# Joining the even and odd key offsets of an attention feature tile in one group of column-tiled matmuls

## The chip, the cores and the metric

The kernel runs on one NeuronCore of a Trainium2 chip. The metric is the device time of one execution in microseconds, as a median over runs. The engines are named as in the profile: PE (TensorE, the matmuls), PEld (its weight loads), DVE (VectorE), ACT (ScalarE), POOL (GpSimd) and SP (SyncE, which issues most DMAs).

## What is computed

Two blocks alternate twice, on x of 2048 positions by 1024 features, each with a residual and a layer norm in front:

```python
x = x + A(layernorm(x))        # attention
x = x + B(layernorm(x))        # MLP over positions
x = x + A(layernorm(x))
x = x + B(layernorm(x))
```

A is attention over a dilated sliding window. It has 32 heads of 32 features, and position s looks at s, s-2, ..., s-14 alone:

```python
qkv = x @ wqkv                                      # [2048, 3*1024]
idx = pos[:, None] - 2 * arange(8)[None, :]         # negative: masked
logits = einsum("bhsd,bhswd->bhsw", q, k[idx]) * 32 ** -0.5
o = einsum("bhsw,bhswd->bhsd", softmax(logits), v[idx])
return o @ wo
```

B mixes positions: u = gelu(h^T w1 + b1) with 3584 hidden units, then y = u w2 + b2, transposed back.

## The kernel before, in words

**Staging.** The window steps by two, so even and odd positions never meet. The kernel splits the positions in two *classes* c of SC = 1024. Each pair of A and B is a *layer* here (li = 0, 1). q, k and v are held transposed, 128 features by 1024 positions: a *feature tile* dt, of which a class has 8. Four feature tiles make a *score group* n, so that a layer has groups 0 to 3 (class 0: 0 and 1; class 1: 2 and 3), and a group is worked on in two halves of two feature tiles.

**Scores, qk() (L434).** There is no matmul of q with k, since every position has its own 8 keys. For a feature tile, DVE multiplies q by four shifted windows of k at once (L444), giving T of 128 x 4096. The 8 offsets need two such products, called *parities* par: one for the even, one for the odd offsets of the window. TensorE then sums the 32 features of each head with a 0/1 matrix sel (L449): 8 matmuls that use 128 rows and 32 columns of the array, four of them side by side (*column-tiled*), for each product. They add into sc, two PSUM banks, one a parity. A *run* in this document is an unbroken sequence of them on PE, with ordinary 128x128 matmuls on either side.

```python
T = tpl.tile([P, 4, SC], BF16, name="T", tag="T")
nc.vector.tensor_tensor(out=T[:], in0=q..., in1=window(k, par, 2, ...), op=ALU.mult)
for sb in range(SB):
    for gr in range(4):
        nc.tensor.matmul(self.sc[32 * gr:32 * gr + 32, par], lhsT=sel[...], rhs=T[...], ...)
```

T shares the two buffers of pool tpl with pr, the intermediate of the value product.

**Softmax and values.** softmax_front() (L453) copies sc to L, adds the mask, takes the maximum and the exponential; softmax_back() (L463) sums, divides (Pb, L470) and writes Pb to DRAM. spread() (L479) reads it back, replicated over the 32 features of a head, as pb, by DMAs on POOL's queue. pv() (L489) multiplies pb by windows of v (L505), adds the 8 offsets (L509, L511), and leaves oT.

**Projections.** proj() (L395) makes a half of q, k or v of a feature tile with 8 matmuls of 128 x 512 (L412); ACT moves the result out of PSUM (L416, L419), k and v into a buffer with a shifted second copy. Weights come through SP's queue: wq tiles with three buffers (pool wqp), and wv, wo, w1 and w2 tiles with five (pool wbp). PSUM has six banks for ordinary products and the two of sc.

**Output projection and MLP.** out_proj() (L611) multiplies oT by wo in 128 x 512 blocks (i: row block, 0 to 7; n: column half), inside multiply() (L631); DVE adds the residual (L652, L655), and ACT or DVE norms the row block into h. Class 0 runs with early = 0, each block finished before the next; class 1 with early = 3: three row blocks are begun with the first six feature tiles and wait in their banks. gemm1() (L672) contracts over positions (L682), for class 0 first as *partials* (kept in the g buffers, L688), later with class 1's half added (L693). gemm2_tile() (L697) makes the output rows (L706), and in between layers also the next layer's normalised hb and its transposed hT.

**Buffers g.** The 14 buffers g0 to g13 hold gemm1's result, 28 hidden tiles, two in a buffer. The last eight, g6 to g13, hold v of class 1 until attention is done. g0 to g5 are 128 x 2048 and idle during the score work of layer 0's groups 1 and 2; g0 to g3 take x rows at the start.

**What sets the order.** Every engine works through a fixed list. The list follows the order in which weave() (L755) asks for units of work. A *lead* stream (stream(), L514) goes through the groups: products and runs, softmax, the next projections, the value products of the group before. *Fills* (second: the class-1 input rows; v_ahead: class 1's v; out0: class 0's output projection; partials, late: gemm1 of class 0) are put in wherever the planner thinks that PE would otherwise wait. The planner keeps two clocks, pe and dve. A unit of kind "dve" adds its cost to dve; if it has a following PE cost, fills are pulled until pe has reached dve. SLACK is 0.5 us; while class 0's output projection is open, a fill is also pulled for every OUT0_GAP = 7 us of DVE work as long as pe < dve + AHEAD. In qk(), a unit is one parity: 2.2 us of DVE, then 0.6 of PE. Instructions of one engine that are given different priorities are ordered by them, so the final list is not exactly the planner's; a wait on PE holds all that is behind it.

Of the kernel before, what the change touches and what calls it, by code (L numbers as in the profile page):

```python
# [11 lines left out]
ALU = mybir.AluOpType  # L12
FP32 = mybir.dt.float32
BF16 = mybir.dt.bfloat16

P = 128
H = 32
DH = 32
W = 8
# [7 lines left out]
def kernel(  # L27
# [13 lines left out]
    nc = tc.nc  # L41
    x_in = A_x[0]
    out2d = out[0]
    S, D = x_in.shape
    F = B_w1.shape[1]
    KD = D // P
# [20 lines left out]
    PB_LAG = 12.0  # L67
    PDW = 4 * SB * W * TB + 512
    OUT0_GAP = 7.0
    AHEAD = 10.0  # L70
    assert D == H * DH and W == 8 and SC == 1024 and HD * KD == H and SB * CH == 32
    scale = float(DH) ** -0.5

# [17 lines left out]
    class at:  # L91
# [8 lines left out]
        def __exit__(self, *a):  # L100
            self.c[0] = tc.cur_priority
            tc.cur_priority = self.old

    tc.cur_priority = 10_000_000
    top = [1_000_000]
# [59 lines left out]
    L = pers.tile([P, W, TB], FP32, name="L")  # L165
    m4 = pers.tile([P, 4, TB], FP32, name="m4")
    Pb = pers.tile([P, W, TB], BF16, name="Pb")
    g_raw = [pers.tile([P, 2 * KW if n >= NFB - KD else GF * D], BF16, name=f"g{n}") for n in range(NFB)]
    g = [t[:, 0:GF * D].rearrange("p (f d) -> p f d", d=D) for t in g_raw]
    v_g = [t[:].rearrange("p (r k) -> p r k", k=KW) for t in g_raw[NFB - KD:]]  # L170

    xa = [[dram.tile([SC, D], BF16, name=f"xa{li}{c}") for c in range(DIL)] for li in range(2)]
    xb = [dram.tile([SC, D], BF16, name=f"xb{c}") for c in range(DIL)]
# [13 lines left out]
    def window(t, par, off, shape):  # L187

        base = t[:, par, off]
        return bass.AP(base.tensor, base.offset, [base.ap[0]] + shape)  # L190
# [161 lines left out]
    class Attn:  # L352

        def __init__(self, li, hT, early):
            self.li, self.hT, self.early = li, hT, early
            self.oT = [[None] * KD for _ in range(DIL)]
            self.wts = {}
            self.pbs = {}

        def v_of(self, c, dt):  # L360
            return v_g[dt] if c else v_t[dt % 2]
# [72 lines left out]
        def qk(self, n, dq):  # L434
            c, dt = n // NCQ, (n % NCQ) * DQ + dq
            if dq == 0:
                self.sc = pssp.tile([P, 2, 4, TB], FP32, name="sc", tag="sc")
            q, k = self.q_of(c, dt), self.k_of(c, dt)
            for par in range(2):
                yield "dve", 2.2, [("ready", 0, dt), ("ready", 1, dt)], [("free", x, dt % 2) for x in range(2)] if par and not self.apart(c, dt) else [], 0.0, 0.6 * bool(n)  # L440
                if n == 0:
                    yield "pe", 0.6, [], [], 0.0
                T = tpl.tile([P, 4, SC], BF16, name="T", tag="T")
                nc.vector.tensor_tensor(out=T[:], in0=q.unsqueeze(1).to_broadcast([P, 4, SC]),  # L444
                                        in1=window(k, par, 2, [(2, 4), (1, SC)]), op=ALU.mult)
                for sb in range(SB):
                    for gr in range(4):
                        b = SB * gr + sb
                        nc.tensor.matmul(self.sc[32 * gr:32 * gr + 32, par], lhsT=sel[:, sb * DQ + dq, :],  # L449
                                         rhs=T[:, :, b * TB:(b + 1) * TB],  # L450
                                         start=(dq == 0 and sb == 0), stop=(dq == DQ - 1 and sb == SB - 1))

        def softmax_front(self):  # L453
            yield "dve", 4.5, [], ["exp"], 1.2, 0.0
# [8 lines left out]
        def softmax_back(self, n):  # L463
            yield "dve", 3.0, ["exp"], [("pb", n, 0)], PB_LAG, 0.0
            yield "dve", 0.0, [], [("pb", n, 1)], PB_LAG + 6.0, 0.0
            nc.vector.tensor_tensor(out=m4[:], in0=L[:, 0:4, :], in1=L[:, 4:8, :], op=ALU.add)
            nc.vector.tensor_tensor(out=m4[:, 0:2, :], in0=m4[:, 0:2, :], in1=m4[:, 2:4, :], op=ALU.add)
            nc.vector.tensor_tensor(out=m4[:, 0, :], in0=m4[:, 0, :], in1=m4[:, 1, :], op=ALU.add)
            nc.vector.reciprocal(out=m4[:, 1, :], in_=m4[:, 0, :])
            nc.vector.tensor_tensor(out=Pb[:], in0=L[:], in1=m4[:, 1:2, :].to_broadcast([P, W, TB]), op=ALU.mult)  # L470
            base = self.pd(n)[0, 0]
            dst = bass.AP(base.tensor, base.offset, [(W * TB, 4 * SB), (PDW, CH), (1, W * TB)])
            nc.gpsimd.dma_start(out=dst, in_=Pb[:].rearrange("p u t -> p (u t)"))
            self.spread(n)
# [136 lines left out]
    def out_proj(at_, c, res, dst, h2, on_act):  # L611

        early = 0 if on_act else 3
        if early:
            yield "pe", 1.28 * early * NDC, [("oT", 0), ("less", "oT", -12.0)], [], 0.0
        dst_v = rows(dst)
        wo_t = [[None, None] for _ in range(NDC)]
        for n in range(NDC):
            for hf in range(2):
                wt = wb("wo", [P, KD // 2, 512])  # L620
                nc.sync.dma_start(out=wt[:], in_=wo_v[hf, :, :, n * 512:(n + 1) * 512])
                wo_t[n][hf] = wt
        for hf in range(2):
            h2[c][hf] = hx(f"h2{c}{hf}", [P, NT // 2, D])
        banks = {}

        def multiply(i, n, kts):
            if (i, n) not in banks:
                banks[(i, n)] = bank()
            for kt in kts:  # L630
                nc.tensor.matmul(banks[(i, n)][:], lhsT=at_.oT[c][kt][:, i * P:(i + 1) * P],  # L631
                                 rhs=wo_t[n][kt // 4][:, kt % 4, :], start=(kt == 0), stop=(kt == KD - 1))

        def kts(i):
            return range(KD - 2 if i < early else 0, KD)

        for i in range(early):
            for n in range(NDC):
                multiply(i, n, range(KD - 2))
        xrs = Rows([res[i] for i in range(NT)], 2)  # L640
        for i in range(NT):
            if early:
                yield "pe", 0.43 * len(kts(i)), ["oT"], [], 3.6
                on_act = i % 2 == 0
            xn = xrs.take()
            s1 = st("s1", [P, NDC]) if on_act else None
            for n in range(NDC):
                cols = slice(n * 512, (n + 1) * 512)
                multiply(i, n, kts(i))
                ps = banks.pop((i, n))  # L650
                if on_act:
                    nc.vector.scalar_tensor_tensor(out=xn[:, cols], in0=ps[:], scalar=1.0, in1=xn[:, cols], op0=ALU.mult,  # L652
                                                   op1=ALU.add, accum_out=s1[:, n:n + 1])
                else:
                    nc.vector.tensor_tensor(out=xn[:, cols], in0=ps[:], in1=xn[:, cols], op=ALU.add)  # L655
            nc.gpsimd.dma_start(out=dst_v[i], in_=xn[:])
            h = h2[c][i // 4][:, i % 4, :]
            if on_act:
                nm, rs = stats_act(xn[:], 1.0 + EPS, eps2, h, s1)
                norm_act(h, xn[:], nm, rs)  # L660
            else:
                mean, rs = stats_dve(xn[:], 1.0 + EPS, eps2)
                norm_dve(h, xn[:], mean, rs)
            if not early:
                yield 3.5, 0.0
# [255 lines left out]
```

## Time and profile before

| | us |
|---|---|
| median of 5 runs | 1292.86 |
| lowest and highest run | 1291.93, 1294.54 |
| the profiled execution's own time | 1292.86 |
| its span (first to last instruction) | 1291.1 |
| outside the span (1292.86 - 1291.1) | 1.76 |

The granted clock of TensorE is 1.00 in the profiled execution. The stages, each with its part of the span and the busy time of the two engines that the change touches:

| stretch, us | what runs | PE busy | DVE busy |
|---|---|---|---|
| 0 to 62 | layer 0: input rows, first projections, first runs | 56.72 | 43.73 |
| 62 to 246 | layer 0: scores, softmax, values, output projection | 179.28 | 172.09 |
| 246 to 395 | layer 0: end of the values, class 1's output projection, gemm1 | 149.00 | 77.17 |
| 395 to 565 | layer 0: gemm1, gemm2 of class 0 | 169.91 | 52.43 |
| 565 to 748 | layer 1: scores of class 0, with gemm2 of class 1 as fill | 179.39 | 129.14 |
| 748 to 885 | layer 1: scores of class 1, output projection of class 0 | 134.73 | 95.57 |
| 885 to 1291 | layer 1: gemm1 and gemm2 | 402.18 | 110.31 |

In the profile's lines, a group or a stretch of the timeline gives start and duration, engine, line, output<-inputs, the tile's shape and a count. An entry in brackets at the end of a timeline line is the idle time just before it, and what ended it. L444 is DVE's product T, L449 the column-tiled sum, L412 a projection, L631 the output projection, L682 gemm1 and L706 gemm2.

### The profile page before, as it was taken

The page shows a single profiled execution, that of the slowest core. Times are in us where ns is not written, and L with a number is a line of the kernel's source. Part 1 is how long each engine was busy: PE and PEld are TensorE (multiplying, and loading weights), DVE is VectorE, ACT ScalarE, POOL GpSimd, SP SyncE. Part 2 cuts the span into 40 slices and gives each one's busy share as a digit, 9 for nine tenths or more (in the row PEclk, how much of TensorE's full clock was granted, in tenths as well). Part 3 has the DMA queues.
Part 4 walks back from the last instruction along what each step waited for, and adds up shares of the span by engine and source line. Part 5 has one row for each costly group of instructions (what it writes and reads, how often), then busy time and mean ns, then how long its engine had stood idle before and what let it go on. Part 6 is the DMA issues. An engine that isn't in the chain of part 4 may idle for free. (4 is left out here: it accounts for less than half of the span.)

```text
span 1291.1 us, 15619 instructions
## 1 busy us (share of the span) xinstructions
PE 1271.2 (98%) x6284; PEld 574.7 (45%) x6284; DVE 680.5 (53%) x861; ACT 502.3 (39%) x836; POOL 60.8 (5%) x166
## 2 busy tenths in 40 slices
PE   8999999999999999999999999999999999999999
PEld 4344444444444444444444444444444444444444
DVE  6879899979013422335896734978930233011011
ACT  6845446634424433325414535484343344000000
POOL 3000001001000000000000000010000000000000
PEclk9999999999999999999999999999999999999999
DMA  9852436563422289953647652349162222334331
GB/s 256 185 122 88 117 106 163 165 153 110 135 82 82 61 223 301 299 143 94 153 121 183 158 141 83 73 138 230 64 181 74 74 82 72 122 120 134 105 112 53
DMA packets 217817, 173.01 MB, mean 134 GB/s; under 512 B 32080, under 2 KB 198352, under 8 KB 215696
## 3 DMA queue, kind: packets, MB, share of 16 engines
q1 hardware_dynamic: 206768, 126.11, 36.6%
q0 software_dynamic: 9248, 37.51, 10.4%
q10 hardware_dynamic: 1728, 8.39, 1.7%
q8 instruction: 49, 0.80, 0.3%
q14 instruction: 24, 0.20, 0.0%
HBM read 139.47 MB, written 26.21 MB: 128 GB/s over the span
## 5 line engine op out<-in xcount | busy, mean ns | idle before, releaser
L706 PE MATMUL ps<-g,w 128*128 128x512 bf16 (+1 forms) x1820 | 390.4, 376 | 1.6 <-ACT v L419 1.6
L682 PE MATMUL ps<-h,w 128*128 128x512 bf16 x1792 | 388.8, 379 | 2.9 <-ACT h L233 2.1
L706 PEld LDWEIGHTS <-w 128*128 128x128 bf16 x1820 | 177.5, 98 | 212.8 <-issue 6.0
L682 PEld LDWEIGHTS <-w 128*128 128x128 bf16 x1792 | 175.0, 98 | 215.8 <-issue 4.6
L412 PE MATMUL ps<-hT,wq 128*128 128x512 bf16 (+1 forms) x1112 | 243.4, 375 | 2.8 <-ACT k L419 1.1
L693 DVE TENSOR_TENSOR tmp<-ps,g 128x512 f32<-128x512 f32 x96 | 66.4, 691 | 210.7 <-PE ps L682 209.6
L444 DVE TENSOR_TENSOR T<-q,k 128x4096 bf16<-128x4096 bf16 x60 | 135.5, 2285 | 64.0 <-ACT q L416 52.5
L711 DVE SCALAR_TENSOR_TENSOR xr<-ps,b_sb,xr 128x512 bf16<-128x512 f32 (+1 forms) x65 | 45.6, 737 | 232.5 <-PE ps L706 200.5
L412 PEld LDWEIGHTS <-wq 128*128 128x128 bf16 x1112 | 108.4, 100 | 132.3 <-issue 13.3
L509 DVE TENSOR_TENSOR pr<-pr 128x2048 bf16<-128x2048 bf16 (+1 forms) x128 | 119.2, 945 | 0.2
L694 ACT ACTIVATE g<-tmp,b_sb 128x512 bf16<-128x512 f32 x96 | 69.2, 721 | 92.9 <-DVE tmp L693 92.5
L412 PE MATMUL ps<-hT,wv 128*128 128x512 bf16 x448 | 101.8, 380 | 0.0
L631 PE MATMUL ps<-wo,oT 128*128 128x512 bf16 x384 | 89.6, 379 | 2.4 <-DMA wo<-in_A_wo_dram 2.4
L688 ACT CAST g<-ps 128x512 bf16<-128x512 f32 x96 | 55.2, 590 | 90.9 <-PE ps L682 90.8
L419 ACT CAST k<-ps 128x1024 bf16<-128x1024 f32 x60 | 60.8, 1015 | 72.9 <-PE ps L412 72.9
L505 DVE TENSOR_TENSOR pr<-pb,v 128x2048 bf16<-128x2048 bf16 x64 | 75.9, 1214 | 21.2 <-DMA pb<-pd 11.1
L505 DVE TENSOR_TENSOR pr<-pb,g 128x2048 bf16<-128x2048 bf16 x64 | 76.3, 1214 | 11.6 <-DMA pb<-pd 11.6
L412 PEld LDWEIGHTS <-wv 128*128 128x128 bf16 x448 | 48.6, 112 | 50.6 <-issue 7.2
L631 PEld LDWEIGHTS <-oT 128*128 128x128 bf16 x384 | 37.3, 98 | 48.8 <-issue 4.7
L416 ACT CAST q<-ps 128x512 bf16<-128x512 f32 x60 | 34.8, 583 | 48.3 <-PE ps L412 48.3
L419 ACT CAST g<-ps 128x1024 bf16<-128x1024 f32 x36 | 36.6, 1016 | 40.9 <-PE ps L412 40.9
L737 ACT COPY odd<-w 128x896 bf16<-128x896 bf16 x32 | 30.0, 937 | 56.5 <-DMA w<-in_B_w_dram 56.4
(91 smaller groups left out, 607.1 us busy)
## 6 DMA issues: line engine op xcount, KB each, us to landing
w<-in_B_w_dram SPq DMA_DIRECT2D x56, 512.0 KB, 4.1
w<-in_B_w_dram SPq DMA_DIRECT2D x64, 448.0 KB, 3.8
wq<-in_A_wqkv_dram SPq DMA_DIRECT2D x38, 512.0 KB, 4.0
pb<-pd POOLq DMA_DIRECT2D x16, 1024.0 KB, 10.3
wo<-in_A_wo_dram SPq DMA_DIRECT2D x16, 512.0 KB, 3.9
xa<-xr POOLq DMA_DIRECT2D x32, 256.0 KB, 3.4
xr<-xa SPq DMA_DIRECT2D x32, 256.0 KB, 3.7
wv<-in_A_wqkv_dram SPq DMA_DIRECT2D x14, 512.0 KB, 5.7
```

The source lines that it names most:

```text
L412: nc.tensor.matmul(ps[:, lo:hi], lhsT=cols, rhs=self.hT[c][hf][:, kt, lo:hi], start=(kt == 0), stop=(kt == KD - 1))
L419: nc.scalar.copy(out=window(buf, 0, PADK + hf * HT, [(KW + 1, 2), (1, HT)]), in_=ps[:].unsqueeze(1).to_broadcast([P, 2, HT]))
L444: nc.vector.tensor_tensor(out=T[:], in0=q.unsqueeze(1).to_broadcast([P, 4, SC]), in1=window(k, par, 2, [(2, 4), (1, SC)]), op=ALU.mult)
L505: nc.vector.tensor_tensor(out=pr[:, :, u, :], in0=pb[:, :, u, :], in1=window(self.v_of(c, dt), par, 2 + hf * HT, [(TB, 4), (2, 4), (1, TB) ...
L509: nc.vector.tensor_tensor(out=pr[:, :, 0:wd, :], in0=pr[:, :, 0:wd, :], in1=pr[:, :, wd:2 * wd, :], op=ALU.add)
L631: nc.tensor.matmul(banks[(i, n)][:], lhsT=at_.oT[c][kt][:, i * P:(i + 1) * P], rhs=wo_t[n][kt // 4][:, kt % 4, :], start=(kt == 0), stop=( ...
L682: nc.tensor.matmul(ps[:], lhsT=wt[c][:, i, fl * P:(fl + 1) * P], rhs=h2[c][i // 4][:, i % 4, dc * 512:(dc + 1) * 512], start=(k == 0), sto ...
L688: nc.scalar.copy(out=gs, in_=ps[:])
L693: nc.vector.tensor_tensor(out=tmp[:], in0=ps[:], in1=gs, op=ALU.add)
L694: nc.scalar.activation(out=gs, in_=tmp[:], func=ACT.Gelu_apprx_tanh, bias=b1_sb[:, ft:ft + 1])
L706: nc.tensor.matmul(ps[:, 0:xc.stop - xc.start], lhsT=w2t(ft, c), rhs=g[ft // GF][:, ft % GF, xc], start=(ft == 0), stop=(ft == FT - 1))
L711: nc.vector.scalar_tensor_tensor(out=xo[:, xc], in0=ps[:, 0:xc.stop - xc.start], scalar=b2_sb[:, i, c:c + 1], in1=xo[:, xc], op0=ALU.add, ...
```

## The change

1. In qk(), except for the first group of layer 0, both parities of a feature tile are multiplied first; then their 16 column-tiled matmuls follow in one group. Its first matmul waits for the second product, and the 16 are chained in order. A helper, follow(), adds such a dependency by hand; Sync is a wait, NoSync only an order within one engine. The products of a layer are chained in order too, and behind the softmax's Pb.
2. The planner sees one unit for the two products (4.5 us of DVE, then 1.1 of PE) instead of two (2.2, then 0.6).
3. g0 to g5 become the halves of three buffers gg0 to gg2, each 128 x 4096. In groups 1 and 2 of layer 0 the products T go to these in turn, instead of into pool tpl.
4. In out_proj() for class 0, column half 0 of the row blocks 0 and 1 is multiplied first; then the order is as before, without these.
5. AHEAD goes from 10 to 5.

In the changed kernel the product T is at L456 and its sum at L480; the lines behind qk() are 32 to 37 higher than before.

```diff
@@ -67,7 +67,7 @@
     PB_LAG = 12.0
     PDW = 4 * SB * W * TB + 512
     OUT0_GAP = 7.0
-    AHEAD = 10.0
+    AHEAD = 5.0
     assert D == H * DH and W == 8 and SC == 1024 and HD * KD == H and SB * CH == 32
     scale = float(DH) ** -0.5
 
@@ -100,6 +100,9 @@
         def __exit__(self, *a):
             self.c[0] = tc.cur_priority
             tc.cur_priority = self.old
+
+    def follow(inst, other, how):
+        tc.add_manual_dep(inst.ins, other.ins.name, mybir.DependencyInfo(how, mybir.DependencyReason.DATA), reason="follow")
 
     tc.cur_priority = 10_000_000
     top = [1_000_000]
@@ -165,9 +168,11 @@
     L = pers.tile([P, W, TB], FP32, name="L")
     m4 = pers.tile([P, 4, TB], FP32, name="m4")
     Pb = pers.tile([P, W, TB], BF16, name="Pb")
-    g_raw = [pers.tile([P, 2 * KW if n >= NFB - KD else GF * D], BF16, name=f"g{n}") for n in range(NFB)]
+    g_two = [pers.tile([P, 2 * GF * D], BF16, name=f"gg{n}") for n in range((NFB - KD) // 2)]
+    g_raw = [t[:, h * GF * D:(h + 1) * GF * D] for t in g_two for h in range(2)]
+    g_raw += [pers.tile([P, 2 * KW], BF16, name=f"g{n}")[:] for n in range(NFB - KD, NFB)]
     g = [t[:, 0:GF * D].rearrange("p (f d) -> p f d", d=D) for t in g_raw]
-    v_g = [t[:].rearrange("p (r k) -> p r k", k=KW) for t in g_raw[NFB - KD:]]
+    v_g = [t.rearrange("p (r k) -> p r k", k=KW) for t in g_raw[NFB - KD:]]
 
     xa = [[dram.tile([SC, D], BF16, name=f"xa{li}{c}") for c in range(DIL)] for li in range(2)]
     xb = [dram.tile([SC, D], BF16, name=f"xb{c}") for c in range(DIL)]
@@ -356,6 +361,7 @@
             self.oT = [[None] * KD for _ in range(DIL)]
             self.wts = {}
             self.pbs = {}
+            self.prior = None
 
         def v_of(self, c, dt):
             return v_g[dt] if c else v_t[dt % 2]
@@ -436,19 +442,45 @@
             if dq == 0:
                 self.sc = pssp.tile([P, 2, 4, TB], FP32, name="sc", tag="sc")
             q, k = self.q_of(c, dt), self.k_of(c, dt)
+            ready = [("ready", 0, dt), ("ready", 1, dt)]
+            free = [] if self.apart(c, dt) else [("free", x, dt % 2) for x in range(2)]
+            joined = n > 0 or self.li > 0
+            if joined:
+                yield "dve", 4.5, ready, free, 0.0, 1.1
+            Ts = []
             for par in range(2):
-                yield "dve", 2.2, [("ready", 0, dt), ("ready", 1, dt)], [("free", x, dt % 2) for x in range(2)] if par and not self.apart(c, dt) else [], 0.0, 0.6 * bool(n)
-                if n == 0:
+                if not joined:
+                    yield "dve", 2.2, ready, free if par else [], 0.0, 0.0
                     yield "pe", 0.6, [], [], 0.0
-                T = tpl.tile([P, 4, SC], BF16, name="T", tag="T")
-                nc.vector.tensor_tensor(out=T[:], in0=q.unsqueeze(1).to_broadcast([P, 4, SC]),
-                                        in1=window(k, par, 2, [(2, 4), (1, SC)]), op=ALU.mult)
-                for sb in range(SB):
-                    for gr in range(4):
-                        b = SB * gr + sb
-                        nc.tensor.matmul(self.sc[32 * gr:32 * gr + 32, par], lhsT=sel[:, sb * DQ + dq, :],
-                                         rhs=T[:, :, b * TB:(b + 1) * TB],
-                                         start=(dq == 0 and sb == 0), stop=(dq == DQ - 1 and sb == SB - 1))
+                T = self.t_buf(n, dq, par)
+                mult = nc.vector.tensor_tensor(out=T, in0=q.unsqueeze(1).to_broadcast([P, 4, SC]),
+                                               in1=window(k, par, 2, [(2, 4), (1, SC)]), op=ALU.mult)
+                Ts.append(T)
+                if joined and self.prior:
+                    follow(mult, self.prior, mybir.DependencyClass.NoSync)
+                self.prior = mult
+                if not joined:
+                    self.qk_sum(dq, par, T)
+            if joined:
+                mms = self.qk_sum(dq, 0, Ts[0]) + self.qk_sum(dq, 1, Ts[1])
+                follow(mms[0], mult, mybir.DependencyClass.Sync)
+                for x, y in zip(mms[1:], mms):
+                    follow(x, y, mybir.DependencyClass.NoSync)
+
+        def t_buf(self, n, dq, par):
+            if self.li == 0 and 0 < n < 3:
+                return g_two[(2 * (n * DQ + dq) + par) % len(g_two)][:].rearrange("p (u t) -> p u t", u=4)
+            return tpl.tile([P, 4, SC], BF16, name="T", tag="T")[:]
+
+        def qk_sum(self, dq, par, T):
+            mms = []
+            for sb in range(SB):
+                for gr in range(4):
+                    b = SB * gr + sb
+                    mms.append(nc.tensor.matmul(self.sc[32 * gr:32 * gr + 32, par], lhsT=sel[:, sb * DQ + dq, :],
+                                                rhs=T[:, :, b * TB:(b + 1) * TB],
+                                                start=(dq == 0 and sb == 0), stop=(dq == DQ - 1 and sb == SB - 1)))
+            return mms
 
         def softmax_front(self):
             yield "dve", 4.5, [], ["exp"], 1.2, 0.0
@@ -467,7 +499,8 @@
             nc.vector.tensor_tensor(out=m4[:, 0:2, :], in0=m4[:, 0:2, :], in1=m4[:, 2:4, :], op=ALU.add)
             nc.vector.tensor_tensor(out=m4[:, 0, :], in0=m4[:, 0, :], in1=m4[:, 1, :], op=ALU.add)
             nc.vector.reciprocal(out=m4[:, 1, :], in_=m4[:, 0, :])
-            nc.vector.tensor_tensor(out=Pb[:], in0=L[:], in1=m4[:, 1:2, :].to_broadcast([P, W, TB]), op=ALU.mult)
+            self.prior = nc.vector.tensor_tensor(out=Pb[:], in0=L[:], in1=m4[:, 1:2, :].to_broadcast([P, W, TB]),
+                                                 op=ALU.mult)
             base = self.pd(n)[0, 0]
             dst = bass.AP(base.tensor, base.offset, [(W * TB, 4 * SB), (PDW, CH), (1, W * TB)])
             nc.gpsimd.dma_start(out=dst, in_=Pb[:].rearrange("p u t -> p (u t)"))
@@ -638,6 +671,9 @@
             for n in range(NDC):
                 multiply(i, n, range(KD - 2))
         xrs = Rows([res[i] for i in range(NT)], 2)
+        if not early:
+            for i in range(2):
+                multiply(i, 0, range(KD))
         for i in range(NT):
             if early:
                 yield "pe", 0.43 * len(kts(i)), ["oT"], [], 3.6
@@ -646,7 +682,8 @@
             s1 = st("s1", [P, NDC]) if on_act else None
             for n in range(NDC):
                 cols = slice(n * 512, (n + 1) * 512)
-                multiply(i, n, kts(i))
+                if early or (i, n) not in banks:
+                    multiply(i, n, kts(i))
                 ps = banks.pop((i, n))
                 if on_act:
                     nc.vector.scalar_tensor_tensor(out=xn[:, cols], in0=ps[:], scalar=1.0, in1=xn[:, cols], op0=ALU.mult,
```

## The prediction

> **What bounds the kernel now.** I read the busy shares first, then the slices, then the groups, and then TensorE's own timeline around every run of column-tiled matmuls.
>
> ```profile
> PE 1271.2 (98%) x6284; PEld 574.7 (45%) x6284; DVE 680.5 (53%) x861; ACT 502.3 (39%) x836; POOL 60.8 (5%) x166
> PE   8999999999999999999999999999999999999999
> DVE  6879899979013422335896734978930233011011
> PEclk9999999999999999999999999999999999999999
> L444 DVE TENSOR_TENSOR T<-q,k 128x4096 bf16<-128x4096 bf16 x60 | 135.5, 2285 | 64.0 <-ACT q L416 52.5
> ```
>
> TensorE is busy 98% of the span at full clock, so the end moves by what TensorE's queue loses or gains, and by nothing else. But VectorE's 53% is a mean over unlike stages: its slices are near full in the first fifth (layer 0) and again near the middle. By stage:
>
> ```profile
> 141.00:162.00 21.00, 21.00 (x108) 9.43 (x109) 21.00 (x21) 9.03 (x12) 0.00 (x0) 1.00 0.29 76
> 162.00:245.00 83.00, 80.59 (x432) 34.08 (x431) 82.34 (x104) 49.73 (x89) 6.02 (x11) 1.00 0.54 153
> 565.00:748.00 183.00, 179.39 (x909) 79.65 (x908) 129.14 (x134) 70.44 (x121) 7.98 (x20) 1.00 0.55 140
> 760.00:820.00 60.00, 60.00 (x339) 25.80 (x338) 35.20 (x24) 28.57 (x33) 1.70 (x3) 1.00 0.38 101
> ```
>
> The columns are the stretch, its length, then PE, PEld, DVE, ACT and POOL busy. In layer 0 (to 245) DVE is as full as PE; in layer 1 it has a third free.
>
> **What a run costs.** In the matmul pitch of 0.216 us (63 matmuls from 772.58 to 786.19), a run shows its price as what is over:
>
> ```profile
> 63.62 7.07 PE L412 MATMUL ps<-hT,wv 128*128 128x512 bf16 x32
> 70.61 1.05 PE L449 MATMUL sc<-T,sel 128*32 128x512 bf16 x16
> 71.59 2.13 PE L412 MATMUL ps<-hT,wv 128*128 128x512 bf16 x9
> ...
> 762.81 3.62 PE L412 MATMUL ps<-hT,wv 128*128 128x512 bf16 x16
> 766.36 0.62 PE L449 MATMUL sc<-T,sel 128*32 128x512 bf16 x8
> 766.90 1.92 PE L412 MATMUL ps<-hT,wv 128*128 128x512 bf16 x8
> ```
>
> 32 full matmuls take 32 x 0.216 = 6.91, and the run starts 6.99 after them; 16 take 3.46, and 3.55 pass. So entry costs 0.09. A run of 8 (four abreast, so two pitches) holds the queue 0.54 to 0.55, 0.12 over its 0.43; one of 16 holds it 0.98, again 0.12 over its 0.86. The overhead is **0.21 us per run, whatever its length**. Where PE also waits 0.04 for T it is 0.25.
>
> **Part 1: fewer runs.** Before has 56 runs (48 of 8, 8 of 16). The changed order has 35, counted in the order of instructions that the build fixes for PE; layer 0's group 0 keeps its seven. That is 21 fewer, with as many matmuls. Summed by stage from before's own excesses (0.21 to 0.25 each, long waits left out): layer 0 n=1,2: 12 runs become 8, 2.80 to 1.67, -1.1. n=3: 8 become 4, 1.87 to 0.84, -1.0. Layer 1 class 0: 14 become 8, 3.44 to 1.67, -1.8. Class 1: 12 become 6, 2.60 to 1.25, -1.35. The last half group: 3 become 2, -0.25. Sum **-5.5**. [...]
>
> **Part 2: the wait for two products.** A joined run must wait for both T's. Two take 4.49 on DVE (one row below), and with two buffers the first can start 0.73 after the previous run's start, when that run has read its first T (70.61 to 71.35; 620.22 to 620.94):
>
> ```profile
> 71.35 4.49 DVE L444 TENSOR_TENSOR T<-q,k 128x4096 bf16<-128x4096 bf16 x2 [0.22 <-PE sc L449]
> ...
> 620.94 4.49 DVE L444 TENSOR_TENSOR T<-q,k 128x4096 bf16<-128x4096 bf16 x2 [4.05 <-PE sc L449]
> ```
>
> So the next run starts no earlier than 0.73 + 4.49 + 0.05 = 5.27 after the last. With 18 full matmuls between, PE is there after 0.98 + 17 x 0.216 + 0.33 = 4.98: it waits 0.29. The order has this three times in layer 1's class 0 and three times in class 1 (+0.87 each), and once in the last half group (+0.25). Lower end: nothing, if PE is late anyway; upper end: doubled, if a pv instruction (1.2) slips between.
>
> In layer 0 three spare buffers remove the buffer's wait, so there the fullness of DVE decides. Behind the waiting run stand all projections of PE's queue, and behind those ACT's evictions; nothing else can go meanwhile. Before already shows such a wait:
>
> ```profile
> 102.47 0.62 PE L449 MATMUL sc<-T,sel 128*32 128x512 bf16 x8
> 105.13 0.62 PE L449 MATMUL sc<-T,sel 128*32 128x512 bf16 x8 [2.04 <-DVE T L444]
> ```
>
> For n=1's second half, the new DVE order puts the fourth product behind three L505 and an L509 of pv (3.50 + 1.22, less 0.17 of overlap = 4.55). Adding this to DVE's order I get its end at 111.0 and PE there at 108.0: a wait of 3.05 in place of 2.2, **+0.85**, and +0.25 at n=1's first run. For n=3, evictions of out_proj (L652, 0.68) now stand between the products; laying DVE's order against PE's gives waits of 1.3, 0.35, 0.95 and 0.4, **+3.0**. Bounds: 0, if DVE runs ahead of me by 1.3, and 6. The pv of group 0 starts earlier: softmax's Pb now precedes the products, 68.1 instead of 71.14, so pb lands about 80 instead of 83.09. This feeds DVE 3 us sooner and is its cushion.
>
> [...] The trace only shows that 2.04 idle left the clock at 1.00.)
>
> **Part 3: other waits that move.** These long waits of PE stand beside the change:
>
> ```profile
> 191.51 7.28 PE L631 MATMUL ps<-wo,oT 128*128 128x512 bf16 x33 [1.86 <-DMA wo<-in_A_wo_dram]
> ...
> 245.26 4.91 PE L682 MATMUL ps<-h,w 128*128 128x512 bf16 x22 [0.72 <-ACT h L233]
> ...
> 630.78 8.81 PE L412 MATMUL ps<-hT,wq 128*128 128x512 bf16 x40 [1.11 <-ACT k L419]
> ...
> 843.19 7.93 PE L631 MATMUL ps<-wo,oT 128*128 128x512 bf16 x36 [0.58 <-DMA wo<-in_A_wo_dram]
> ...
> 874.23 6.85 PE L682 MATMUL ps<-h,w 128*128 128x512 bf16 x31 [1.04 <-ACT h L233]
> ```
>
> At 191.51 the fourth wo tile, issued on SP, queues behind the last use of a wv buffer. Now out_proj starts with both blocks' column tile 0, 16 matmuls (3.5) that need only the first two wo tiles, and that last v projection comes about 12 us earlier: the wait of 2.0 (with its restart) goes, **-2.0**. The same reorder covers 843.19: **-0.75**. At 245.26, and 240.5, gemm1 waits for normalised rows; PE gets there later and the evictions on DVE are done earlier, **-1.1**. At 630.78 PE waited for a wq load (ACT was long done); the planner's new order puts 14 gemm2 matmuls (3.0) in front: **-1.27**. At 874.23 and 881.44 (0.52) the last out_proj evictions come some 5 us sooner in DVE's order, for -1.7; since ACT's four norms behind them are not sped up, I take half, **-0.85**. DMAs: none is added; wo's four loads move ahead of nothing that waits. The other loads' stalls (675.57 and 711) stay.
>
> AHEAD 10 to 5 and the planner's costs show only in the orders. They spend 98 instead of 56 gemm2 matmuls before layer 1's first softmax, leaving 112 instead of 168 for the end. The cushion of pv there (DVE's end of pv to the fill's end) falls from 17.7 to 5.6 us. I cost it at nothing while those 5.6 hold.
>
> **Sum.** -5.5 + 0.85 + 0.25 + 3.0 + 0.87 + 0.87 + 0.25 - 2.0 - 0.75 - 1.1 - 1.27 - 0.85 = -5.4. From the profiled execution's 1292.86 (span 1291.1; also the median of the runs): **1287.4**.
>
> **Rivals.**
> 1. Better: PE finds every product ready; the +6.1 of new waits shrink to about 1.5, 1283. For: before's second runs waited 0.04 only. Against: DVE is full to 245. Chance 0.09.
> 2. The waits that go come back elsewhere (a load or a row is late by its own queue): 630, 874, 843 and 245 stay (+4.0), 1291.4, no change. For: a load's arrival doesn't depend on the score runs, and PE arrives sooner by the runs saved. Chance 0.24. That the runs don't shrink falls under it: the static order has the 35.
> 3. Slower: **VectorE becomes the pacemaker of layer 0.** A joined run is held by its second product; DVE, full from 83, can't catch up, and each lateness passes to PE and back to the next projections. The price is the lateness of pv's start beyond the plan: cushion 4.3 us, so it decides once pb lands over some 21 us after Pb rather than 12 to 13, or once n=3's waits reach 12 rather than 3; each further us adds one. At 9 more: 1296.4. For: 21.00 of 21.00 busy in the stretch from 141. Against: the cushion. Chance 0.12.
>
> **Numbers.** Forecast 0.55 (1285 to 1290.2). 0.2%, about what a measurement can tell from none, is 2.6 us: faster under 1290.3, slower over 1295.4. Faster 0.55 + 0.09 = 0.64, same 0.24, slower 0.12. The range reaches from rival 1 to past rival 2: 1283.0 to 1293.0, leaving out rival 3 and tails.
>
> **What would show it.** Right: 35 runs with 0.21 each; PE's wait at n=1's fourth product near 3 us; n=3's waits summing to 3; nothing at out_proj's start; gemm1's first rows without waits. Wrong: a run of 16 that costs more than 0.21; T waits of over 6 in layer 0; PE stalls in layer 1's class 0 at oT or at loads that before did not have; a clock under 1.00.

## The result, and the profile after

| | before | changed |
|---|---|---|
| median, us | 1293.72 (42 runs) | 1296.66 (22 runs) |
| lowest and highest | 1291.88, 1298.59 | 1293.66, 1298.56 |
| profiled execution, its span | 1292.86, 1291.1 | 1298.6, 1296.8 |
| mean granted clock of the profiled execution | 1.00 | 0.997 |

The ratio of the changed kernel to before is 1.002, with an interval of 1.0014 to 1.0026: slower by some 2.6 us, where 5.4 less had been forecast. The profiled execution of the changed kernel is one of its longer ones; its span is 5.7 over that of before, so the sums by profile further down explain 5.7 and not 2.6.

The page's busy times, slices and product group, as they now stand:

```profile
PE 1269.1 (98%) x6284; PEld 578.1 (45%) x6284; DVE 680.9 (53%) x861; ACT 499.8 (39%) x836; POOL 60.7 (5%) x166
PE   8999899999999999999999999999999999999999
DVE  6799799977303322234796944798850243011011
L456 DVE TENSOR_TENSOR T<-q,k 128x4096 bf16<-128x4096 bf16 x44 | 99.3, 2284 | 72.5 <-ACT q L422 54.3
```

Nothing here tells of a loss: PE is as busy as before, and T takes 2.28 us as before. (44 products are in pool tpl; the other 16 go to the g buffers and stand in a group of their own.) The loss shows only in PE's timeline, run by run. A run itself costs what was predicted:

```profile
854.77 6.21 PE L664 MATMUL ps<-wo,oT 128*128 128x512 bf16 x28
860.90 1.05 PE L480 MATMUL sc<-T,sel 128*32 128x512 bf16 x16
861.88 4.28 PE L664 MATMUL ps<-wo,oT 128*128 128x512 bf16 x19
```

28 x 0.216 = 6.05, and 6.13 pass; the run holds the queue 0.98: 0.21 over its matmuls' time. The 35 runs cost 7.3 us where the 56 of before cost 11.7. But two of them wait for long. First group 1's second half, where the run of 16 at 111.17 waits for the fourth product:

```profile
104.27 1.05 PE L480 MATMUL sc<-gg,sel 128*32 128x512 bf16 x16
105.25 1.92 PE L418 MATMUL ps<-hT,wv 128*128 128x512 bf16 x8
107.00 1.24 PE L418 MATMUL ps<-hT,wq 128*128 128x512 bf16 x5
111.17 1.90 PE L480 MATMUL sc<-gg,sel 128*32 128x512 bf16 x16 [2.93 <-DVE gg L456]
113.00 5.26 PE L418 MATMUL ps<-hT,wq 128*128 128x512 bf16 x20
```

The wait of 2.93 was in the forecast (3.05). What follows it was not: the run of 16 takes 1.90 instead of 1.05, and the 20 matmuls behind it 5.26, where 20 x 0.216 + 0.16 would be 4.5. The first of them start 0.43 apart. Then group 2's first half:

```profile
142.15 1.05 PE L480 MATMUL sc<-gg,sel 128*32 128x512 bf16 x16
143.13 3.64 PE L418 MATMUL ps<-hT,wv 128*128 128x512 bf16 x16
150.91 1.05 PE L480 MATMUL sc<-gg,sel 128*32 128x512 bf16 x16 [4.14 <-DVE gg L456]
151.89 6.39 PE L418 MATMUL ps<-hT,wq 128*128 128x512 bf16 x21
```

This wait of 4.14 is in no step of the prediction, and it too has matmuls at half pace behind it. VectorE's timeline of both places tells why the product came late:

```profile
104.17 3.48 DVE L538 TENSOR_TENSOR pr<-pb,v 128x2048 bf16<-128x2048 bf16 x3
107.69 1.23 DVE L542 TENSOR_TENSOR pr<-pr 128x2048 bf16<-128x2048 bf16 x1
108.83 2.28 DVE L456 TENSOR_TENSOR gg<-q,k 128x4096 bf16<-128x4096 bf16 x1
...
143.90 3.50 DVE L538 TENSOR_TENSOR pr<-pb,v 128x2048 bf16<-128x2048 bf16 x3 [7.87 <-DMA pb<-pd]
147.43 1.22 DVE L542 TENSOR_TENSOR pr<-pr 128x2048 bf16<-128x2048 bf16 x1
148.57 2.28 DVE L456 TENSOR_TENSOR gg<-q,k 128x4096 bf16<-128x4096 bf16 x1
```

In both, the fourth product of the half group stands behind three L538 and an L542 of the value product. At the second, those wait themselves: VectorE sits idle for 7.87 us until pb lands, with the product that PE needs next in line behind them. For most of that time the product could not have started either, since it reuses the first product's buffer, which the run at 142.15 reads. In pf_group2 (experiment 2), where nothing else is ahead of it, it starts 0.67 after that run does (140.96 after 140.29). So here it could have started at about 142.8, and starts at 148.57: 1.1 of the 5.8 are the rest of the idle time, 4.7 the value products. Without them it would have ended near 145.1, before PE is there at 146.8. VectorE is not full there; the product is held by its place in the order.

The granted clock, from a table of stretches (PEclk is the third number from the end):

```profile
107.78:111.19 3.41, 0.48 (x7) 0.02 (x6) 3.41 (x3) 0.44 (x1) 0.00 (x0) 1.00 0.10 32
111.20:114.55 3.35, 3.35 (x20) 1.02 (x21) 3.35 (x6) 1.06 (x2) 0.00 (x0) 0.50 0.00 0
114.65:116.00 1.35, 1.35 (x8) 0.64 (x7) 1.35 (x4) 0.87 (x1) 0.00 (x0) 1.00 0.00 0
...
150.50:156.00 5.50, 5.09 (x28) 1.89 (x29) 5.50 (x8) 0.69 (x1) 0.00 (x0) 0.69 0.00 0
```

So the clock is half from 111.19 to 114.6 and full on both sides. Before has 1.00 in both places (107 to 116 and 146 to 156). By the starts of the matmuls, the half pace costs 0.85 + 0.78 = 1.63 us behind the first wait and 1.65 behind the second.

In layer 1 the score runs wait as forecast, but other waits have grown (before, the wait for hT was 0.28 and that for gemm1's first rows 1.04):

```profile
725.45 3.61 PE L418 MATMUL ps<-hT,wq 128*128 128x512 bf16 x16 [1.06 <-DVE xr L748]
728.90 0.38 PE L743 MATMUL ps<-gg,w 128*128 128x512 bf16 x1
730.70 5.12 PE L743 MATMUL ps<-gg,w 128*128 128x512 bf16 x23 [1.42 <-ACT v L425]
...
763.62 6.63 PE L418 MATMUL ps<-hT,wq 128*128 128x512 bf16 x30 [1.89 <-DMA hT<-hb]
...
881.72 3.40 PE L719 MATMUL ps<-h,w 128*128 128x512 bf16 x15 [1.64 <-ACT h L238]
```

### The profile page after: what moved, and what is told of

Same layout as the page of the kernel before. It is cut to its first block, busy times and chain, and to the rows that moved or that the text cites. A ratio compares the mean times of both kernels' runs of the same rounds, so it can differ in the third digit from the quotient of the medians.

```text
span 1296.8 us, 15594 instructions
## 1 busy us (share of the span) xinstructions
PE 1269.1 (98%) x6284; PEld 578.1 (45%) x6284; DVE 680.9 (53%) x861; ACT 499.8 (39%) x836; POOL 60.7 (5%) x166
## 3 DMA queue, kind: packets, MB, share of 16 engines
q0 software_dynamic: 9248, 37.51, 10.4%
## 5 line engine op out<-in xcount | busy, mean ns | idle before, releaser
L743 PE MATMUL ps<-g,w 128*128 128x512 bf16 (+1 forms) x1040 | 227.6, 376 | 0.0
L743 PE MATMUL ps<-gg,w 128*128 128x512 bf16 (+1 forms) x780 | 172.0, 376 | 1.4 <-ACT v L425 1.4
L456 DVE TENSOR_TENSOR T<-q,k 128x4096 bf16<-128x4096 bf16 x44 | 99.3, 2284 | 72.5 <-ACT q L422 54.3
L542 DVE TENSOR_TENSOR pr<-pr 128x2048 bf16<-128x2048 bf16 (+1 forms) x128 | 119.2, 946 | 0.3
L730 DVE TENSOR_TENSOR tmp<-ps,gg 128x512 f32<-128x512 f32 x48 | 33.2, 691 | 150.3 <-PE ps L719 150.3
L538 DVE TENSOR_TENSOR pr<-pb,v 128x2048 bf16<-128x2048 bf16 x64 | 76.0, 1214 | 25.9 <-DMA pb<-pd 15.3
L538 DVE TENSOR_TENSOR pr<-pb,g 128x2048 bf16<-128x2048 bf16 x64 | 76.2, 1215 | 13.8 <-DMA pb<-pd 12.5
L730 DVE TENSOR_TENSOR tmp<-ps,g 128x512 f32<-128x512 f32 x48 | 33.2, 691 | 49.7 <-PE ps L719 48.7
L731 ACT ACTIVATE gg<-tmp,b_sb 128x512 bf16<-128x512 f32 x48 | 34.6, 722 | 49.9 <-DVE tmp L730 49.9
```

The source lines that it names most:

```text
L456: mult = nc.vector.tensor_tensor(out=T, in0=q.unsqueeze(1).to_broadcast([P, 4, SC]), in1=window(k, par, 2, [(2, 4), (1, SC)]), op=ALU.mult)
L538: nc.vector.tensor_tensor(out=pr[:, :, u, :], in0=pb[:, :, u, :], in1=window(self.v_of(c, dt), par, 2 + hf * HT, [(TB, 4), (2, 4), (1, TB) ...
L542: nc.vector.tensor_tensor(out=pr[:, :, 0:wd, :], in0=pr[:, :, 0:wd, :], in1=pr[:, :, wd:2 * wd, :], op=ALU.add)
L730: nc.vector.tensor_tensor(out=tmp[:], in0=ps[:], in1=gs, op=ALU.add)
L731: nc.scalar.activation(out=gs, in_=tmp[:], func=ACT.Gelu_apprx_tanh, bias=b1_sb[:, ft:ft + 1])
L743: nc.tensor.matmul(ps[:, 0:xc.stop - xc.start], lhsT=w2t(ft, c), rhs=g[ft // GF][:, ft % GF, xc], start=(ft == 0), stop=(ft == FT - 1))
```

## The experiments

The theories: **A**, the order on VectorE (the fourth product behind the value products) costs the two waits, and **A1**, the half clock follows from them; **B**, VectorE is the pacemaker of layer 0, so a wait taken away comes back; **C**, the planner's new costs spoil layer 1. Times are medians, with the ratio to before on the same chip.

### 1. The products first

```diff
+                    if self.li == 0 and n < 2 and dqs == (0,):
+                        follow(first, self.prior, mybir.DependencyClass.NoSync)
```

("first" is an L538 of pv(), prior the half group's last product: an order on VectorE, no wait. It holds in both halves of score groups 1 and 2.)

> The changed kernel, with the value products of layer 0's groups 0 and 1 ordered on VectorE behind the four products T of the half group. Theory A (order): the changed kernel loses its gain at two places, where the fourth product stands behind three L538 and one L542 (waits of 3.0 and 4.2 us, each followed by some 1.6 us at half clock). Both waits fall to about 0.3 and the granted clock is 1.00: 1286 to 1288. Theory B (VectorE is the pacemaker of layer 0): the wait only moves to the next run or to the value products, at least 1293. Theory C (the plan of layer 1 is what costs): these places matter only for their own waits without the clock, about 1290.

Measured: **1286.71** (1286.32 to 1286.89), ratio 0.9937 (0.9921 to 0.9954), clock 1.00 in every run. PE and, below it, VectorE:

```profile
106.99 0.38 PE L418 MATMUL ps<-hT,wq 128*128 128x512 bf16 x1
107.30 1.05 PE L480 MATMUL sc<-gg,sel 128*32 128x512 bf16 x16
108.28 4.92 PE L418 MATMUL ps<-hT,wq 128*128 128x512 bf16 x22
...
142.08 1.05 PE L480 MATMUL sc<-gg,sel 128*32 128x512 bf16 x16
143.06 7.30 PE L418 MATMUL ps<-hT,wq 128*128 128x512 bf16 x33
```

```profile
104.93 2.29 DVE L456 TENSOR_TENSOR gg<-q,k 128x4096 bf16<-128x4096 bf16 x1 [0.73 <-PE sc L480]
107.14 1.22 DVE L538 TENSOR_TENSOR pr<-pb,v 128x2048 bf16<-128x2048 bf16 x1
...
138.19 2.29 DVE L456 TENSOR_TENSOR gg<-q,k 128x4096 bf16<-128x4096 bf16 x1 [1.52 <-PE sc L480]
140.40 3.49 DVE L538 TENSOR_TENSOR pr<-pb,v 128x2048 bf16<-128x2048 bf16 x3
```

The fourth product starts as soon as its buffer is read, and neither run waits any more. 1296.66 - 1286.71 = 9.95, where A's terms are 3.0 + 4.2 + 1.6 + 1.6 = 10.4. B falls. Once more, beside the changed kernel on one chip:

> The changed kernel itself, on the same chip as the three that follow, as their base: 1296 to 1297.5.

> products_first once more, on the chip of changed_again: 1286 to 1287.5, 9 to 11 us under it.

Measured: 1297.12 (ratio 1.0009, 0.9997 to 1.0021; on this chip before had 1294.84) and **1286.51** (0.9931, 0.9917 to 0.9946).

### 2. Each place by itself

products_first with `n == 1` in place of `n < 2`, so that only group 2's products come first:

> products_first with the products put first in group 2 alone; group 1's second half keeps the changed kernel's order on VectorE. Theory A: of the 10 us between the changed kernel and products_first, group 2's wait (4.2) and the half clock behind it (1.6) are 5.8, group 1's wait (3.0) and its half clock (1.6) are 4.2 to 4.6: 1290.5 to 1291.5, with one wait of 3 us near 111. Rival (the two are one effect, the second wait only follows from the first being late): 1286 to 1288, or 1295 and over.

Measured: **1290.74** (0.9977, 0.9968 to 0.9987). The wait near 111 stayed (2.81), the one near 151 was gone. Group 2's place is worth 5.9 (A's terms: 5.8), and what is left to products_first, group 1's, 4.0 (A's terms: 4.2 to 4.6), so the rival of a single effect falls. Group 1's order alone was not run: it is not shown that group 2's wait would stay without group 1's.

### 3. No common wait

```diff
-                follow(mms[0], mult, mybir.DependencyClass.Sync)
```

> The changed kernel without the wait of a run's first matmul for the second product; only the matmuls that read that product wait for it, and the scheduler may put other matmuls between (43 runs by the built order instead of 35, 8 x 0.21 = 1.7 us). Theory A: the waits at the fourth products of groups 1 and 2 (3.0 and 4.2) and the half clock behind them go, as do the small waits of about 0.3 in layer 1: 1285 to 1288, clock 1.00. Theory B: at least 1293, since the products come no sooner. Theory C: about 1290.

Measured: **1296.93** (1.0014, 1.0001 to 1.0027): a miss for A as I had put it. PE:

```profile
107.09 0.61 PE L479 MATMUL sc<-gg,sel 128*32 128x512 bf16 x8
107.64 0.61 PE L418 MATMUL ps<-hT,wq 128*128 128x512 bf16 x2
111.44 0.87 PE L479 MATMUL sc<-gg,sel 128*32 128x512 bf16 x8 [3.19 <-DVE gg L456]
```

The first 8 matmuls run at once, and the wait stands in front of the other 8, with the half clock behind it (0.66 as the mean of 111 to 116). The same happens at group 2's place (a wait of 2.38 in front of 150.20). VectorE's order is the same, three products with pb and one sum (L537 and L541 here) ahead of the product. At these places it is not the common wait of a run that costs; it is when the fourth product comes.

### 4. The clock

Eight matmuls whose result nothing reads are put into the two long waits, released by small memsets on GpSimd; the waits remain. The first form:

> The changed kernel, with 14 matmuls of 128x512 added (their results are used by nothing) inside the two long waits of layer 0, released one pair after the other by small memsets on GpSimd, so that no idle time of TensorE there is longer than about 1.7 us. The waits themselves stay. Theory A1 (the half clock behind the waits is a consequence of the idle time and costs 1.6 us at each): no rows at half clock behind 111 and 151, clock 1.00, 1293 to 1294.5. Rival (the idle time alone is the cost, the clock is not): 1296 to 1297.5, as the changed kernel.

Measured: **1305.75** (1.0084, 1.007 to 1.0097). It tells nothing of the two places: I had taken the wait near 151 for group 2's second half, so the memsets delayed a run that had not waited (to 188.56), and the memsets followed each other 0.17 us apart, not the 0.105 I had counted with, so that the run near 111 came 2.4 late too. The mended form:

```diff
+            if self.li or (n, dq) not in ((1, 3), (2, 1)):
+                return []
+            for i in range((24, 39)[n - 1]):
+                m = nc.gpsimd.memset(nap[:], 0.0)
...
+                    d = nc.tensor.matmul(ps[:], lhsT=ident[:], rhs=T[:, 0, 0:512], start=True, stop=True)
```

> A mended form of kept_awake: eight 128x512 matmuls inside each of the two long waits of the changed kernel (group 1's second half, and group 2's first half, where the first form had missed the place), released in pairs by small memsets of 0.17 us on GpSimd, so that TensorE is never idle for more than about 1.3 us there. VectorE's order is that of the changed kernel. In group 1 five projection matmuls (1.1 us) stand behind the run instead of before it, so 1.1 us are added. Theory A1 (half clock follows from the idle time and costs some 3.2 us in all): clock 1.00 behind both waits, 1296.7 + 1.1 - 3.2 = 1294.6, and 1293.5 to 1295.5. Rival (the idle time alone is the cost): 1297 to 1299.

Measured: **1295.02** (1.0016, 1.0005 to 1.0027), and 0.999 to 1.00 as the clock of all 11 runs, where 10 of changed_again's 12 had 0.996 or 0.997. PE near 111:

```profile
109.39 0.61 PE L484 MATMUL ps<-gg,ident 128*128 128x512 bf16 x2 [0.42 <-POOL nap L479]
110.88 1.05 PE L501 MATMUL sc<-gg,sel 128*32 128x512 bf16 x16 [0.89 <-DVE gg L457]
111.86 8.38 PE L419 MATMUL ps<-hT,wq 128*128 128x512 bf16 x37
```

The product is as late as before, the run takes 1.05 again, and the 37 matmuls keep their pitch. The time is 1.6 under the changed kernel although 1.1 was added: 2.7 for the clock, for which the rows gave 3.3. The time alone is a weak witness, since the two ratios' intervals overlap (1.0005 to 1.0027, and 1.0014 to 1.0026 for the changed kernel); the clock of the runs and the rows are the strong one. The best witness is the changed kernel itself. In changed_again the profiled execution had waits of 3.00 and 3.54 at the two places and no half clock:

```profile
111.00:116.00 5.00, 5.00 (x35) 2.13 (x36) 5.00 (x9) 2.95 (x3) 0.00 (x0) 1.00 0.00 0
...
148.44 1.05 PE L480 MATMUL sc<-gg,sel 128*32 128x512 bf16 x16 [3.54 <-DVE gg L456]
149.42 8.81 PE L418 MATMUL ps<-hT,wq 128*128 128x512 bf16 x40
```

and took 1293.19. (The first row is from its table of stretches, the others from PE's timeline; the wait of 3.00 is before 110.92. Its profile holds no record of the clock's changes, so the pace is the evidence: 40 x 0.216 + 0.16 = 8.80, and 8.81 were taken.) Over the 35 runs of the changed kernel, the three at clock 1.00 took 1293.19, 1293.66 and 1294.53, the 27 at 0.996 or 0.997 took 1295.5 to 1298.6. Why the same wait brings the half clock in one execution and not in another was not shown.

### 5. The planner, AHEAD and the output projection

> The changed kernel with AHEAD back at 10; the order differs only near the end of layer 1's attention (output projection of class 0). Theory A and B: within 1 us of the changed kernel (1295.7 to 1297.7). Theory C: the wait for normalised rows at the start of gemm1 (1.8 us in the changed kernel) shrinks, 1293 to 1295.

Measured: **1298.93** (1.0031, 1.002 to 1.0041), a miss for both: no gain but a loss. The second wait for gemm1's normalised rows grew from 0.38 to 1.06, and a third of 1.59 appeared. So AHEAD = 5 is no part of the loss; that it is a gain, of 1 to 2 us, is likely but not shown, since the intervals of the two ratios overlap and the profiled spans differ by 0.9.

The old costs in layer 1, in the changed kernel and in products_first:

```diff
-                yield "dve", 4.5, ready, free, 0.0, 1.1
+                if self.li:
+                    yield "dve", 2.2, ready, [], 0.0, 0.6
+                    yield "dve", 2.2, ready, free, 0.0, 0.6
+                else:
+                    yield "dve", 4.5, ready, free, 0.0, 1.1
```

> The changed kernel with the planner's old costs in layer 1 and nothing else (the products of layer 0 keep the changed order). Theory C in its smaller form (the plan of layer 1 costs 2 to 3 us, beside the 10 of the order on VectorE): 1293.5 to 1295 where the changed kernel has 1296.7. Rival (the waits of layer 1 only move, and the lower time of pf_costs was another chip's): within 0.7 us of changed_again.

> products_first with the planner's old costs in layer 1 (two units of 2.2 and 0.6 instead of one of 4.5 and 1.1); the fill left for the end of class 0's attention is 140 matmuls instead of 112. Theory C (the plan of layer 1 uses its fill up too early): the waits there, 1.3 and 1.6 for ACT's evictions of v and 1.9 for the last transposed rows, shrink by 2 to 3 in all, 1284 to 1285. Rival (the waits only move): 1286 to 1288.

Measured: **1294.67** (0.9995, 0.9985 to 1.0006), 2.4 under changed_again, and **1284.15** (0.9928, 0.9915 to 0.9942), the lowest time of all. The intervals of the first ratio and of changed_again's overlap, but the two ran on one chip and can be compared at the same clock: at 0.996 or 0.997 its nine runs took 1293.5 to 1296.2, changed_again's ten 1295.8 to 1298.6. PE at the end of class 0's attention in pf_costs:

```profile
741.39 7.07 PE L418 MATMUL ps<-hT,wq 128*128 128x512 bf16 x31
748.66 7.07 PE L418 MATMUL ps<-hT,wq 128*128 128x512 bf16 x32 [0.20 <-issue]
```

The wait of 1.89 for hT is down to 0.20, and those of 1.06 and 1.42 are gone. In their place the load's wait at 631.51 (1.42 over the pitch) is back, and gemm1 waits 0.90 for a load of w at 940.51, as before did at 949. The spans are 1282.3 and, for products_first, 1285.0.

The output projection's new order, alone in before, taken out of products_first, and taken out with the old costs:

> Before, with nothing but the new order of class 0's output projection (column half 0 of row blocks 0 and 1 first). The prediction's term: the waits for the fourth wo tile (2.0 in layer 0, 0.75 in layer 1) go, 1291.0, a ratio of 0.998. Rival (the load is late by its own queue, so the wait comes back behind the 16 matmuls, or the later blocks lose what the first gain): 1293 to 1294, no change.

> products_first without the new order of class 0's output projection. If the reorder is worth the waits for wo that it covers (2.0 in layer 0, 0.75 in layer 1): 1289 to 1290. Rival (most of it comes back at other waits, as out_proj_alone gave 0.9 with an interval that holds nothing): 1286.5 to 1288.

> Products first, old planner costs in layer 1, and the old order of class 0's output projection. If the plan of layer 1 is worth 2 to 3 us and the reorder nothing: 1283.5 to 1285, 2 to 3 us under products_first_again. Rival (neither matters): 1286 to 1287.5.

Measured: **1293.91** (0.9994, 0.9979 to 1.0009); **1285.58** (0.994, 0.9928 to 0.9953); **1285.23** (0.9919, 0.9905 to 0.9933). The reorder is worth nothing that these runs can tell, and taking it out of products_first loses nothing. pf_no_reorder has no wait for wo in layer 0 at all, and 0.68 in layer 1, in place of which the wait for normalised rows is 0.91 instead of 1.46. The last is 1.3 under products_first_again on its chip, with no run in common, but it changes the costs and the reorder at once. So the planner's new costs lose some 2.4 us in the changed kernel, as C had it; behind the new order on VectorE the loss is likely but not settled (pf_costs is 2.4 under products_first_again by time and 0.0003 by ratio).

### 6. Buffers and joining

products_first with `if False:` in t_buf(), so that T is always in tpl; with the 8 matmuls after each product, unchained; and pf_costs without the common wait in group 3:

> products_first with the products T of layer 0's groups 1 and 2 in pool tpl again, as before the change, instead of the g buffers. Theory A: the third buffer is needed; with two, a joined run starts 5.27 us after the last, while 8 to 16 matmuls between take 3 to 4.5 us, so that four runs wait 1 to 2.3 us each: 1291 to 1296. Rival (VectorE is full there in any case, the buffer does not matter): 1286 to 1288.

> products_first without the joining: each product's 8 matmuls follow it with no chain and no common wait, and the scheduler puts them where it sees fit (42 runs by the built order instead of 35). If the joining is what gains: 7 more runs at 0.21 cost 1.5 us, the waits for second products give back at most that, 1286.5 to 1288.5. Rival (the order of the products on VectorE gains, the joining nothing or less, since its waits eat it): 1283.5 to 1286.

> pf_costs (products first, old planner costs in layer 1) without the run's wait for its second product in group 3 of both layers, where products stand between evictions of the output projection; 40 runs by the built order instead of 35. If those waits (2.4 us in layer 0, 0.6 in layer 1) are the next to go and five runs cost 1.05: 1282 to 1283.5. Rival (the evictions set the start in any case): 1284 to 1285.5.

Measured: **1288.26** (0.9953, 0.9941 to 0.9965), **1287.09** (0.9945, 0.9933 to 0.9956) and **1284.92** (0.9933, 0.992 to 0.9945). The third buffer is worth some 1.5 us at most (the ratio's interval overlaps that of products_first), far less than its expectation: the scheduler puts more matmuls between the runs (17 instead of 9 between those at 104.63 and 109.92), so that the waits are 0.23. Joining or not joining makes 0.4 of a difference, which is within the intervals: 7 more runs cost about what the waits for second products give back. Of the 21 runs that went, 14 are gone without the joining too (42 runs instead of 56). In group 3 the rival holds: a looser wait gains nothing.

## Why the prediction was wrong, step by step

The runs' price and most of the waits that were costed came out near their size; one wait was overlooked, and the clock was kept at 1.00. (The recorded sum, -5.38, gives 1287.5 rather than 1287.4, which changes nothing.)

- **Runs**: 21 fewer. Their price fell from 11.7 to 7.3, so -4.4. The other 1.1 of my 5.5 were short waits for T inside them; I should have counted these as waits, which come back.
- **Waits for two products in layer 1**: forecast 0.87 + 0.87 + 0.25 = 1.99, measured 1.9. Right.
- **Group 1's second half**: forecast 3.05, measured 2.93. Right.
- **Group 3**: forecast 3.0, measured 2.0. Right in kind.
- **Group 2's first half**: the step that failed. I had laid VectorE's order against PE only where VectorE was busy ("there the fullness of DVE decides"), and had taken pv's start as given. Here VectorE is idle, waiting for pb, and the product stands behind the waiting value products: 4.14 that no term holds. The question to ask, who is queued behind an instruction that waits for a DMA, was asked of PE and SP, and not of VectorE.
- **The clock**: the second step that failed. I kept 1.00, because "2.04 idle left the clock at 1.00". That was one wait in one execution, and it does not speak for others: 2.93 and 4.14 had the half clock behind them here, 3.00 and 3.54 in changed_again did not. The half clock cost 1.63 + 1.65 in the profiled execution, and some 3 in most (27 of the 35 runs have 0.996 or 0.997).
- **Waits that go**: wo at 191.51 (2.0) and 843.19 (0.75) and the load at 630.78 (1.27) did go, but the reason given for the first was wrong: in pf_no_reorder it goes without the reorder as well. The rows at 240.5 and 245.26 gave 0.4 of 1.1, and those at 874 and 881 grew by 0.45 in place of -0.85.
- **Back elsewhere**: 711 and 712 grew by 0.9, 755.90 by 1.6, 309 and 568 by 1.1; 949 gave back 0.95. The planner's costs, put at nothing "while those 5.6 hold", were wrong for the waits near 711 and 755: with 112 instead of 168 fill matmuls left there, v's evictions and hT's last rows come onto the path. With the old costs the wait for hT is gone, and 2.4 us of the time with it (costs_alone).

By the profile: -4.4 for the runs, +8.5 for waits in front of and inside them (the half clock left out), +3.3 for the clock, -1.1 for all other waits make +6.3, where the spans differ by 5.7. The rest is in gaps under the 0.23 us that were counted. Rival 3 named the place (layer 0, VectorE, the start of pv) but not the mechanism: by its rule pb's landing counts only beyond some 21 us after Pb, and here it came 15.4 after Pb's end (128.5 to 143.9). The work on VectorE was not too much either: products_first, with as much of it, gave 1286.7, 0.7 below the forecast. That the forecast sum and this time agree is partly chance, since group 1's wait, in the forecast, is gone in it.

## What to carry to other kernels

When two instructions are made to wait as one, look up where the second of them stands in its own engine's list, and whether anything ahead of it waits for a DMA: an engine that is idle by the profile may still be blocked. A gain that is spread over many runs (21 x 0.21) is undone by two waits; putting one product ahead of four value instructions at these two places made 10 us of difference, and the joining itself 0.4. And a wait of PE costs more than its length once the clock follows it (2.93 and 4.14 had 1.63 and 1.65 more behind them); compare executions by their granted clock before comparing their times: at 1.00 the changed kernel took 1293.2 to 1294.5, before 1291.5 to 1294.5 beside it.

## What the runs showed of the hardware

In the profiled execution of the changed kernel the clock fell to 0.50 behind waits of 2.93 and 4.14, from 111.19 to 114.60 and from 152.15 to 155.56. It also fell behind 3.19 in wait_in_run (its run of 8 taking 0.87 instead of 0.62) and behind 2.52 in kept_awake (0.72 as the mean of 108 to 114); and in out_proj_alone a wait of 1.66 behind one of 0.26 had it, its run of 8 at 40.41 taking 1.02 instead of 0.62. In other profiled executions 2.81 (pf_group2) and 3.00 and 3.54 (changed_again) left the runs of 16 behind them at 1.05, their length at clock 1.00; and in before, at 1.00 throughout, a wait of 1.66 had a run of 8 of 0.61 behind it at 40.05. So the length of a wait does not decide alone; what else does was not shown. (The ends of matmuls are modelled in the profile, so the hundredths are uncertain.) In kept_awake2, where the spare matmuls left no wait over 0.89 at the two places, the clock was 1.00 at both.

The times of before go with the clock too: beside changed_again its runs at clock 1.00 took 1291.5 to 1294.5, those at 0.997 took 1296.3 to 1298.7. What stands ahead of the drop there was not seen, since its profiled execution has none. products_first, in which neither of the two waits is left, spread over 0.6 us in five runs at clock 1.00 (1286.32 to 1286.89); one of six runs of products_first_again, at 0.999, took 1288.21 where the others took 1286.2 to 1286.6.
